# A two-layer attention and MLP kernel: the first unit's maxima one quad further ahead, the second unit's rows in another room

## The chip, the cores and the metric

The kernel runs on one core of one Trainium2 chip. The metric is the device time of one execution in microseconds (us); the kernel before is shown by the median of its timed runs. Five engines work side by side, each through its own instructions in order: TensorE (PE; its weight loads are shown as PEld), VectorE (DVE), ScalarE (ACT), GpSimd (POOL) and SyncE (SP), which here only issues DMAs. ACT issues the DMAs of the weights.

## The reference

The input has 2048 rows of 640 numbers. The same two blocks are applied twice, with the same weights both times:

```python
x = x + attention(layernorm(x), wqkv, wo)     # 32 heads of 20, sliding window of 256 keys
x = x + mlp(layernorm(x), w1, b1, w2, b2)     # 640 -> 1536 -> 640
```

In the attention, q, k and v are the three thirds of `x @ wqkv`. Scores are q.k / sqrt(20); a query sees its own position and the 255 before it; the softmax is taken over these, its weighted sum of v is formed, and the heads together are multiplied by `wo`. In the MLP, `h = x @ w1 + b1`, negative values become zero, the rest is squared, and `h @ w2 + b2` is the result. All is float32.

## The kernel before

**Units.** The 2048 rows are cut into 8 groups of 256 (`T`), and with two layers there are 16 units (`NU`), worked through in order. For a unit u the work is: layernorm of its 256 rows (two blocks of 128), q and k (`stage_qk`) and v (`stage_v`), the attention in eight "quads" of four heads, the projection by `wo` (`stage_o`), the second layernorm, and the MLP (`stage_f`). The first unit of a layer has no earlier keys and uses "whole" quads (`whole_quad`); the others use "half" quads (`halves_quad`).

**Numbers as pairs.** A float32 operand of a large matrix multiplication is kept as two float16 parts, high and low, and three products are added (`mm3`, line 339). Every result that becomes an operand again is therefore evicted twice: ACT writes the high part, then DVE writes the low part (lines 534 and 537 for q and k). The weights are split in the same way when they have been loaded (lines 271 and 272).

**The quads.** For each quad four passes of TensorE alternate:
- "m" (`max_quad`): scores, of which DVE takes the maximum over the keys (lines 717, 720; lines 683 for whole quads);
- "r" (`max_out`): the maxima of two quads are turned by TensorE and written by SP into two extra rows of q (line 757), so that they are subtracted inside the next scores;
- "s" (`exp_quad`): the scores again, now less their maximum; ACT takes the exponential (line 825), and POOL and DVE clear what lies outside the window;
- "v" (`pv_quad`): the weighted sum of v (line 931), copied out by ACT (line 943), for half quads added up by DVE (line 946), and written to device memory every second quad (line 951).

m and s share the same banks of the accumulation memory. The large multiplications ("dense" work) use two other banks; a new one waits until a bank's eviction is done. `load_o` reads a unit's attention result back from device memory (lines 984, 985), divides by the row sums (1017, 1020), and splits it (1024, 1027) for `stage_o`.

**Trips.** q and k of a unit go from their evicted form (`qd`) to device memory (`leave`, lines 583 and 585) and back in another layout (line 589).

**Rows of the next units.** A layernormed block has to be turned for the projections. `split_t` does it with TensorE transposes (line 403) and two evictions (lines 389, 390). `cross` does it with two casts (ACT line 452, DVE line 456) and DMA transposes issued by SP (line 459). Before the change units 1 and 2 go by `cross` (`ln_early`).

**Rooms.** Several tiles share memory over time. `hraw` (name stg) is the room that holds the MLP's hidden values later; at first it has two sides of equal size, side 0 and side 1. `kts[2]`, later the k of unit 2, holds at first some of the loaded `wqkv`, then unit 1's turned rows (`place`), then the second-layer MLP weights `w2` as they come in, five places in all, two of them elsewhere. The tile "qd" is one room for several purposes. Before the change the loads of `w2` into `kts[2]` wait for `gate2`, which opens once v of unit 1 has been computed.

**The order of the work.** The kernel writes its order out by hand with a small planner in Python, which runs while the program is built. Each instruction off TensorE is a `Job` with an engine, an assumed cost, earlier jobs it needs and an urgency (a lower number goes first). The planner keeps an assumed clock per engine and places a job on its engine when it could start (`pump`). The urgencies are in the dictionary `urgency`: `od` the split of the attention result, `ln` the layernorms of `stage_o`, `turn` the maxima, `exp` and `clear` the exponentials and clearing of half quads, `y` and `cross` the ways of the turned rows, `out` the evictions. "Bulk" jobs, the loads of `wo`, `w1` and `w2` on ACT, are also paced by what DMA is assumed to be under way (`moved`).

For unit 0 the function `flow` takes a list of passes (`todo`) and draws dense work from the generator `ahead_all` (units 0 to 2: q, k, v) whenever the next pass isn't ready. What is then left of `ahead_all` is worked off in unit 1. From unit 1 on, `together` lays the dense work of a unit between its quads: the projections of unit u + 1, `stage_o` and `stage_f` of unit u - 1. In the last two units some dense work is held back (`CARRY` from unit 14 into 15, `KEEP` past the quads of unit 15) to cover the last trip of the attention result. `LEAD` is 3: the maxima run three quads ahead.

The core of the old order, lines 1364 to 1366:

```python
todo = [("m", n) for n in range(GQ)] + [("r", 0)] + [("m", n) for n in range(GQ, LEAD)]
for n in range(NQ):
    todo += [("s", n)] + ([("r", n + LEAD - GQ)] if n % GQ == 1 else []) + [("m", n + LEAD), ("v", n)]
```

with `GQ` = 2 and `NQ` = 8.

Of the kernel before, what the change touches and what calls it, by code (L numbers as in the profile page):

```python
# [16 lines left out]
P = 128  # L17
# [28 lines left out]
def kernel(ctx: ExitStack, tc: tile.TileContext, x, wqkv, wo, w1, b1, w2, b2, out):  # L46
# [71 lines left out]
    TAIL = {"A": 115.0, "D": 85.0, "G": 40.0, "S": 0.0}  # L118

    class Job:  # L120
        def __init__(self, eng, cost, fn, deps, nb, prio, size=0, idle=False, land=LAND):
# [4 lines left out]
        def ready(self):  # L126
            return all(d.end is not None for d in self.deps)

        def start(self):
            t = max([clk[self.eng], self.nb] + [d.end + LAT for d in self.deps])  # L130
            return max(t, moved[0] - 2200.0) if self.idle else t

# [186 lines left out]
    def load_w2():  # L319
        used_by = {}  # L320
        for c, place in enumerate((3, 4, 0, 1, 2, 0, 1, 2, 0, 1, 2, 0)):
            first = [w1j[f] for f in (c // 4 * 2, c // 4 * 2 + 1, 6 + c // 4 * 2, 7 + c // 4 * 2)]
            st = vts[1 + place][1][:, :D] if place > 2 else krow[2][:, D * place:D * (place + 1)]
            load = bulk(lambda st=st, c=c: nc.scalar.dma_start(st, w2[c * P:(c + 1) * P, :]), P * D * 4,
                        *([w2j[used_by[place]]] if place in used_by else [gate] if place > 2 else [gate, gate2]))
            w2j[c] = convert(st, w2_s[:, 0, c], w2_s[:, 1, c], D, load, *first)
            used_by[place] = c
        sums.extend(post("D", 130, lambda i=i: set_sums(4 + i), w2j[used_by[3 + i]], prio=2) for i in range(2))

    urgency = {"out": 0, "od": 1, "cross": 1, "mask": 0, "turn": 1, "exp": 1, "ln": 1, "y": 0.5, "clear": 0.5}

# [108 lines left out]

    def cross(ys, dst, room, prio=2):

        box = {}
        js, out, j = [], [], None
        for i, (y, ready) in enumerate(ys):
# [12 lines left out]

            j = post("A", 615, high, ready, j, prio=prio)
            out.append(dma(lambda turn=turn: turn(0), P * D * 2, j, cost=1250.0, land=CROSS))
# [4 lines left out]
    def ln_early(u, place=None):  # L467

        def dst():
            yTs[u] = place  # L470
            if place is None:
                yTs[u] = sb.tile([P, 2, KC, T], F16, name="yT", tag="yT", bufs=1)
            return yTs[u]

        pre[u] = cross(lns.pop(u), dst, lambda: hraw[:, KC * T:2 * KC * T].bitcast(F16).rearrange(
            "p (i a n) -> p i a n", i=2, a=2), 1)
        left["side1"] = ((0, -u), pre[u], [])

# [23 lines left out]
    def stage_qk(u, which=(0, 1)):  # L502
# [9 lines left out]
        for j, c0 in order:  # L512
            if j not in qds:
                if j == 0:
                    qts[u] = sb.tile([P, NP, T], F16, name="qt", tag="qt", bufs=2)
                if j and u < 2:
                    qd, k = side(0), "side0"
                elif u == 2 and not j and opened0:
                    qd, k = side(1), "side1"
                elif j and u > 2:  # L520
                    qd = beside(u)[:, 1].rearrange("p (c a n) -> p c a n", a=2, n=T)
                    k = None
                else:
                    qd, k = sb.tile([P, KC, 2, T], F16, name="qd", tag="qd", bufs=1), "qd"
# [15 lines left out]
            def evict(wait, k=k, n=n, c0=c0, high=high, low=low, jobs=jobs, j=j, dst=dst, qd=qd):  # L540
                pr = urgency["out"]
                old = left.get(k, ())
                if k and (j, u) != old[:1]:
                    old = left[k] = ((j, u), [], old[1] if old else [])
# [28 lines left out]
    def leave(u, j, dst, qd, ready, c0, n):  # L573
# [17 lines left out]

        wrote = dma(write, n * P * 3 * T * 2, ready, n=2, prio=0)

# [375 lines left out]
    def load_o(u, late=False, free_=()):  # L969
# [16 lines left out]

        loaded = dma(load, P * (KC + 1) * T * 4, *wrote, *free_, n=2, prio=0)
        if u == NU - 1:
            both = sb.tile([P, 2, D], F32, name="x1", tag="qt", bufs=2)
# [308 lines left out]

    QKC, VC, OC, FCST, LNC, CARRY, KEEP, MID = 16.4e3, 8.2e3, 8.2e3, 39.2e3, 1.2e3, 18e3, 24e3, 10e3

    def flow(todo, dense):
# [3 lines left out]
        while todo:  # L1305
# [19 lines left out]
            elif kind == "s":  # L1325
                quad = exp_quad(n)
            else:
                pv_quad(n, quad)
            pump()
# [17 lines left out]

    place = kts[2].rearrange("p a n -> p (a n)")[:, :2 * KC * T].rearrange("p (a c n) -> p a c n", a=2, n=T)

    def ahead_all():  # L1350
        yield from stage_qk(0)
        ln_early(1, place)
        yield from stage_v(0, range(2))
        ln_load(2)
        yield from stage_v(0, range(2, 4))
        ln_early(2)
        yield from stage_qk(1)
        yield from stage_v(1)
        gate2.end = now[0]
        yield from stage_qk(2)  # L1360
        yield from stage_v(2)

    rest = ahead_all()
    todo = [("m", n) for n in range(GQ)] + [("r", 0)] + [("m", n) for n in range(GQ, LEAD)]
    for n in range(NQ):
        todo += [("s", n)] + ([("r", n + LEAD - GQ)] if n % GQ == 1 else []) + [("m", n + LEAD), ("v", n)]
    flow(todo, rest)
# [3 lines left out]
    while not all(j.end is not None and j.end <= now[0] + LOOK for j in bbjobs):  # L1371
        c = next(rest)
        if not isinstance(c, Want):
            used[0] += c
            step(c)
    left_over = 3 * (QKC + VC) - used[0]
    rate[0] = 320.0
    for u in range(1, NU):
        last = u == NU - 1
        if u == 1:  # L1380
            urgency.update({"out": 0, "od": 1.5, "cross": 1, "mask": 0, "turn": 0.7, "exp": 0.7, "ln": 0.5, "y": 1, "clear": 0.5})
        quads, ahead = range(NQ * u, NQ * (u + 1)), range(NQ * u + LEAD, NQ * (u + 1) + LEAD)
# [46 lines left out]
```

## Time and profile before

| | us |
|---|---|
| timed runs | 1559.91, 1560.23, 1561.74 |
| median | 1560.23 |
| the profiled execution | 1561.46 |
| its span, first to last instruction | 1559.6 |
| TensorE busy in the span | 1533.5 |
| DVE busy | 1043.3 |
| ACT busy | 669.7 |
| POOL busy | 451.8 |

The span is that of the instructions; the profiled execution's time has 1.9 us more around it. The mean granted clock of TensorE is 0.997. Rows of the timeline read: start, duration, engine, line, operation, what is written from what, shapes, how many instructions were merged (x), and in brackets the idle time of the engine before it and what ended that. Rows of a table by stretch read: from:to, length, then for TensorE, its weight loads, DVE, ACT and POOL the busy time with the number of instructions, the granted clock, the DMA engines' share and GB/s. Rows of the waits read: who waited for whom, the total in us, how often, and the longest.

### The profile page before, as it was taken

The numbers are of one execution on the slowest core, as the hardware profiler recorded it, in microseconds if no ns is written. First come the engines' busy times: TensorE is split into PE (matmuls) and PEld (weight loads), VectorE is DVE, ScalarE is ACT, GpSimd is POOL, SyncE is SP. The second block draws the span as 40 slices with busy tenths as digits, with TensorE's granted clock in tenths as the row PEclk, the third lists the DMA queues.
The fourth block names the chain that finished last, engine by engine and source line by source line (L and its number), as shares of the span: only waits on it lengthen the run. The fifth ranks groups of instructions, "written<-read, shape, count | busy, mean of one in ns | idle before, by whom it ended". The sixth has DMA issues, their size and how long they took to land. (4 is left out here: it accounts for less than half of the span.)

```text
span 1559.6 us, 58897 instructions
## 1 busy us (share of the span) xinstructions
PE 1533.5 (98%) x25822; PEld 1198.6 (77%) x25822; DVE 1043.3 (67%) x2244; ACT 669.7 (43%) x1365; POOL 451.8 (29%) x847
## 2 busy tenths in 40 slices
PE   8998999999999999999999999999999999999999
PEld 6666778787787877878777787877878777786777
DVE  8878775666757667675666757667675676667642
ACT  4565435334453443435343453444435335354422
POOL 1223314232141331413224141321413214142412
PEclk9999999999999999999999999999999999999999
DMA  9975354352534424344462434425243342542120
GB/s 271 209 201 127 80 121 92 106 114 54 123 88 114 105 74 126 69 126 89 99 130 63 119 91 119 100 70 132 67 126 89 94 117 65 122 90 59 30 68 18
DMA packets 248745, 162.16 MB, mean 104 GB/s; under 512 B 96552, under 2 KB 232232, under 8 KB 248488
## 3 DMA queue, kind: packets, MB, share of 16 engines
q1 hardware_dynamic: 242120, 148.89, 38.7%
q10 hardware_dynamic: 6368, 9.50, 2.1%
q8 instruction: 202, 3.31, 0.9%
q14 instruction: 55, 0.45, 0.1%
HBM read 84.68 MB, written 52.95 MB: 88 GB/s over the span
## 5 line engine op out<-in xcount | busy, mean ns | idle before, releaser
L825 ACT ACTIVATE pt<-bb 128x640 f32<-128x640 f32 (+2 forms) x512 | 311.9, 684 | 167.6 <-PE bb L840 148.9
L854 POOL TENSOR_SCALAR_AFFINE_SELECT pt<-pt 64x256 f32<-64x256 f32 x448 | 199.3, 445 | 582.1 <-ACT pt L825 560.0
L339 PE MATMUL acc<-y,w_s 128*128 128x256 f16 x2880 | 330.2, 274 | 1.2 <-DVE y L390 1.2
L339 PE MATMUL acc<-w_s,hh 128*128 128x320 f16 (+1 forms) x2340 | 326.7, 297 | 0.1
L339 PEld LDWEIGHTS <-w_s 128*128 128x128 f16 x2880 | 276.4, 98 | 40.9 <-issue 2.0
L339 PEld LDWEIGHTS <-hh 128*128 128x128 f16 x2340 | 222.1, 98 | 86.8 <-issue 0.4
L720 DVE TENSOR_REDUCE mx<-bb 128x4 f32<-128x1024 f32 x224 | 273.2, 1224 | 6.8
L339 PE MATMUL acc<-yT,wq_s 128*128 128x256 f16 x2250 | 259.1, 273 | 3.0 <-DVE qd L537 1.2
L339 PEld LDWEIGHTS <-wq_s 128*128 128x128 f16 x2400 | 229.6, 98 | 37.3 <-issue 4.3
L863 DVE COPY_PREDICATED_SCALAR pt<-drop,zero 128x256 f32 x224 | 99.9, 497 | 134.3 <-ACT pt L825 133.8
L1130 DVE TENSOR_TENSOR hh<-r,hh 128x256 f16<-128x256 f32 x192 | 98.3, 525 | 110.8 <-ACT hh L1127 105.7
L931 PE MATMUL pv<-pt,vt 64*32 64x192 f32 (+5 forms) x3840 | 166.7, 302 | 0.9 <-DVE y L390 0.6
L943 ACT COPY ot<-pv 128x256 f32<-128x256 f32 x128 | 47.6, 372 | 276.1 <-PE bb L931 247.2
L1124 POOL TENSOR_TENSOR r<-r 128x256 f32<-128x256 f32 x192 | 121.9, 655 | 127.9 <-ACT r L1120 125.3
L931 PE MATMUL bb<-pt,vt 64*32 64x128 f32 (+3 forms) x3584 | 153.5, 301 | 0.0
L717 DVE COPY_PREDICATED bb<-maskq,bb 128x256 f32<-128x256 uint16 x224 | 93.8, 423 | 85.7 <-PE bb L703 80.0
L931 PEld LDWEIGHTS pv<-pt,vt 64*32 64x32 f32 (+1 forms) x3840 | 125.5, 106 | 31.7 <-issue 3.7
L339 PE MATMUL acc<-wo_s,od 128*128 128x320 f16 x960 | 139.6, 299 | 2.2 <-ACT od L1024 2.0
L339 PE MATMUL acc<-wq_s,yT 128*128 128x320 f16 x900 | 132.1, 302 | 5.0 <-DVE qd L537 4.2
L1120 ACT ACTIVATE r<-acc,b1s 128x256 f32<-128x256 f32 x192 | 81.1, 476 | 98.6 <-PE acc L339 96.5
L339 PEld LDWEIGHTS <-od 128*128 128x128 f16 x960 | 90.9, 98 | 40.6 <-ACT od L1024 2.3
L339 PEld LDWEIGHTS <-yT 128*128 128x128 f16 x900 | 87.1, 98 | 40.0 <-issue 6.2
(103 smaller groups left out, 1476.3 us busy)
## 6 DMA issues: line engine op xcount, KB each, us to landing
qt<-qk SPq DMA_DIRECT2D x30, 480.0 KB
kt<-qk SPq DMA_DIRECT2D x30, 480.0 KB
o<-ot SPq DMA_DIRECT2D x256, 42.0 KB
qk<-qd SPq DMA_DIRECT2D x15, 640.0 KB
od<-o SPq DMA_DIRECT2D x14, 640.0 KB
qk<-yl SPq DMA_DIRECT2D x13, 640.0 KB
xt<-in_A_x_dram SPq DMA_DIRECT2D x16, 320.0 KB
x<-in_A_x_dram SPq DMA_DIRECT2D x16, 320.0 KB
```

What stands on the lines that cost most here:

```text
L339: nc.tensor.matmul(acc, lhs(a, c), rhs(b, c), start=(k == 0), stop=(k == 3 * nk - 1))
L717: nc.vector.copy_predicated(wins[:, :, 4 * Q:], later, wins[:, :, :Q])
L720: nc.vector.tensor_reduce(most, wins[:, :, Q:], axis=mybir.AxisListType.X, op=ALU.max)
L825: return lambda: nc.scalar.activation(room_of(box)[:, a:b], bank[:, a:b], AF.Exp, scale=SCALE / (QS * QS))
L854: nc.gpsimd.affine_select(out=m, in_=m, pattern=[[0, 4], [-1 if k else 1, Q]], base=0, fill=0.0, compare_op=ALU.is_gt if k else ALU.is_ge, ...
L863: nc.vector.copy_predicated(m, drop[:, k:k + 1, :].bitcast(mybir.dt.uint16).to_broadcast([P, 4, Q]), zero.unsqueeze(1).to_broadcast([P, 4, ...
L931: nc.tensor.matmul(pv[h][32 * jj:32 * (jj + 1), q0 * Q:(q0 + w) * Q], vf[r, c:c + 32], boxes[e]["pt"][r, a:b], start=(k == 0), stop=(k == ...
L943: nc.scalar.copy(ot[:, qd % 2], to)
L1120: nc.scalar.activation(box["r"], acc[:, f, :], AF.Relu, bias=b1s[:, f0 + f:f0 + f + 1], scale=1.0 / (YS * WS))
L1124: nc.gpsimd.tensor_tensor(box["r"], box["r"], box["r"], op=ALU.mult)
L1130: nc.vector.tensor_sub(hh[:, 1, f, :], box["r"], hh[:, 0, f, :])
```

## The change

- In unit 0 the maxima run four quads ahead instead of three (m0 to m3 and two "r" before s0; none beside the last quad); "r" follows "v".
- Unit 1's rows are turned by TensorE (`ln_t`) between two halves of v of unit 0, and lie in side 1 of `hraw` instead of `kts[2]`. The rows of unit 2 still go by `cross`, now through the "qd" room.
- Q of unit 2 uses side 0 instead of side 1 of `hraw`, where it comes before the attention result of unit 0 is loaded.
- The loads of `w2` into `kts[2]` wait for the split of `wqkv` instead of `gate2`.
- `quiet`: from the last "v" of unit 0 until its attention result has been loaded, the planner issues no bulk load and no write of unit 2's q and k.
- K of unit 1 is asked for after Q of unit 1 and the casts of unit 2.
- The urgencies are other ones, and their update comes at unit 2 instead of unit 1; `CARRY` and `KEEP` are 20 and 28 instead of 18 and 24.

```diff
+    quiet = []
...
         def ready(self):
-            return all(d.end is not None for d in self.deps)
+            return all(d.end is not None for d in self.deps) and not (self.idle and any(q.end is None for q in quiet))
...
-            return max(t, moved[0] - 2200.0) if self.idle else t
+            return max([t, moved[0] - 2200.0] + [q.end for q in quiet]) if self.idle else t
...
-                        *([w2j[used_by[place]]] if place in used_by else [gate] if place > 2 else [gate, gate2]))
+                        *([w2j[used_by[place]]] if place in used_by else [gate] if place > 2 else [gate, *wqj.values()]))
...
-    urgency = {"out": 0, "od": 1, "cross": 1, "mask": 0, "turn": 1, "exp": 1, "ln": 1, "y": 0.5, "clear": 0.5}
+    urgency = {"out": 0, "od": 1, "cross": 2, "mask": 0, "turn": 1, "exp": 0.5, "ln": 1, "y": 0.5, "clear": 0}
...
-            j = post("A", 615, high, ready, j, prio=prio)
+            j = post("A", 615, high, ready, j, *free_, prio=prio)
...
-        pre[u] = cross(lns.pop(u), dst, lambda: hraw[:, KC * T:2 * KC * T].bitcast(F16).rearrange(
-            "p (i a n) -> p i a n", i=2, a=2), 1)
-        left["side1"] = ((0, -u), pre[u], [])
+        pre[u] = cross(lns.pop(u), dst, lambda: sb.tile([P, 2, 2, D], F16, name="yl", tag="qd", bufs=1), 1, left["qd"][1])
+        left["qd"] = ((0, -u), pre[u], [])
...
                 elif u == 2 and not j and opened0:
-                    qd, k = side(1), "side1"
+                    qd, k = side(0), "side0"
...
-        wrote = dma(write, n * P * 3 * T * 2, ready, n=2, prio=0)
+        wrote = dma(write, n * P * 3 * T * 2, ready, *(quiet if u == 2 else ()), n=2, prio=0)
...
+        if u == 0:
+            loaded.gates.append(quiet[0])
...
-    QKC, VC, OC, FCST, LNC, CARRY, KEEP, MID = 16.4e3, 8.2e3, 8.2e3, 39.2e3, 1.2e3, 18e3, 24e3, 10e3
+    QKC, VC, OC, FCST, LNC, CARRY, KEEP, MID = 16.4e3, 8.2e3, 8.2e3, 39.2e3, 1.2e3, 20e3, 28e3, 10e3
...
+                if n == NQ - 1:
+                    quiet.append(Job("S", 0.0, None, [], 0.0, 0))
                 pv_quad(n, quad)
...
-    place = kts[2].rearrange("p a n -> p (a n)")[:, :2 * KC * T].rearrange("p (a c n) -> p a c n", a=2, n=T)
+    place = hraw[:, KC * T:2 * KC * T].bitcast(F16).rearrange("p (a c n) -> p a c n", a=2, n=T)

     def ahead_all():
         yield from stage_qk(0)
-        ln_early(1, place)
         yield from stage_v(0, range(2))
-        ln_load(2)
+        yield from ln_t(1, place)
+        ln_load(2, prio=1)
         yield from stage_v(0, range(2, 4))
+        yield from stage_qk(1, (0,))
         ln_early(2)
-        yield from stage_qk(1)
+        yield from stage_qk(1, (1,))
         yield from stage_v(1)
-        gate2.end = now[0]
         yield from stage_qk(2)
         yield from stage_v(2)
...
-    todo = [("m", n) for n in range(GQ)] + [("r", 0)] + [("m", n) for n in range(GQ, LEAD)]
+    todo = [("m", n) for n in range(GQ)] + [("r", 0)] + [("m", n) for n in range(GQ, LEAD + 1)] + [("r", GQ)]
     for n in range(NQ):
-        todo += [("s", n)] + ([("r", n + LEAD - GQ)] if n % GQ == 1 else []) + [("m", n + LEAD), ("v", n)]
+        m = n + LEAD + 1
+        todo += [("s", n)] + [("m", m)] * (n < NQ - 1) + [("v", n)] + [("r", m)] * (m % GQ == GQ - 1 and n < NQ - 1)
...
-        if u == 1:
-            urgency.update({"out": 0, "od": 1.5, "cross": 1, "mask": 0, "turn": 0.7, "exp": 0.7, "ln": 0.5, "y": 1, "clear": 0.5})
+        if u == 2:
+            urgency.update({"out": 0, "od": 1, "cross": 0.5, "mask": 0, "turn": 0.5, "exp": 0.5, "ln": 1, "y": 1, "clear": 0.5})
```

More of the change, by code (lines that the diff above doesn't have):

```diff
@@ L441, in ln_t, with cross @@
             yield from split_t(ys[i][0], yT[:, :, :, i * P:(i + 1) * P], ys[i][1], pre[u], bb[i])
-    def cross(ys, dst, room, prio=2):
+    def cross(ys, dst, room, prio=2, free_=()):
         box = {}
@@ L542, in evict @@
                 old = left.get(k, ())
-                if k and (j, u) != old[:1]:
+                if k and (not old or old[0] != (j, u)):
                     old = left[k] = ((j, u), [], old[1] if old else [])
@@ L1375 @@
             step(c)
-    left_over = 3 * (QKC + VC) - used[0]
+    left_over = 3 * (QKC + VC) + LNC - used[0]
     rate[0] = 320.0
```

## The prediction

> **What bounds the kernel now.** I read the page's busy table first, then who TensorE waited for, in two stretches, and then the granted clock where the waits lie.
>
> ```profile
> span 1559.6 us, 58897 instructions
> PE 1533.5 (98%) x25822; PEld 1198.6 (77%) x25822; DVE 1043.3 (67%) x2244; ACT 669.7 (43%) x1365; POOL 451.8 (29%) x847
> ```
>
> TensorE is busy for 98% of the span. Whatever the diff does elsewhere, it can only win where TensorE waits or is clocked down. The waits of TensorE from 20 to 165 us (the three longest), and after "..." from 165 to 1400 us (those of 0.5 us or more):
>
> ```profile
> PE acc L339 <- DVE qd L537: 5.3, 3, 4.2
> PE tr L403 <- DVE xt L378: 1.8, 1, 1.8
> PE bb L840 <- DVE ot L946: 1.3, 1, 1.3
> ...
> PE bb L840 <- issue: 2.3, 3, 1.1
> PE bb L703 <- ACT pt L825: 0.9, 2, 0.7
> PE acc L339 <- DVE yl L537: 0.5, 2, 0.3
> ```
>
> The second group sums to 3.7 us over 1235 us: units 2 to 13 are full, and the diff can hardly win there. The first group has 8.4 us in 145 us. The clock (the number after the five engines' busy times; DMA share and GB/s follow) shows two further losses:
>
> ```profile
> 34.60:38.00 3.40, 3.40 (x16) 1.98 (x15) 2.27 (x14) 0.44 (x1) 0.00 (x0) 0.55 1.00 241
> 140.40:147.20 6.80, 6.44 (x63) 4.71 (x63) 5.77 (x12) 3.93 (x7) 2.24 (x2) 0.52 0.10 18
> ```
>
> From 34.6 to 38.0 us the clock is 0.55, which loses 3.4 x 0.45 = 1.5 us; from 140.4 to 147.2 it is 0.52, which loses 6.8 x 0.48 = 3.3 us. Each follows a stretch in which TensorE stood: the longest wait for L537 (4.2 us, up to 33.06 by a row below), and the 1.8 us wait for L378 with its neighbours. So two stalls hold what can be won: **stall 1** 4.2 + 1.5 = 5.7 us, **stall 2** 1.8 + 1.3 + 3.3 = 6.4 us.
>
> **The change part by part.** The sum is made against the profiled execution's own 1561.46 us (its span of 1559.6 and 1.9 around it), which is 1.23 us above the median of the three timed runs, 1560.23; I carry the difference over to the median.
>
> *Stall 1: unit 1's rows leave the DMA path.* The rows of ACT, DVE, TensorE and SP, in this order, at that place:
>
> ```profile
> 31.09 0.72 ACT L452 CAST stg<-xt 128x640 f16<-128x640 f32 x1 [2.76 <-DVE xt L378]
> 31.72 0.38 ACT L534 ACTIVATE qd<-acc 128x256 f16<-128x256 f32 x1
> ...
> 30.44 0.61 DVE L378 TENSOR_SCALAR xt<-xt,bmv 128x640 f32<-128x640 f32 x1 [0.44 <-POOL bmv L376]
> ...
> 32.59 0.42 DVE L537 SCALAR_TENSOR_TENSOR qd<-acc,qd 128x256 f16<-128x256 f32 x1
> ...
> 33.06 0.70 PE L339 MATMUL acc<-wq_s,yT 128*128 128x320 f16 x4 [4.18 <-DVE qd L537]
> ...
> 28.35 4.69 SPq L459 DMA_TRANSPOSE kt<-stg x3
> ```
>
> V's first matmul (33.06) needs a bank, whose eviction is the ACT half L534 and then the DVE half L537. L534 stands behind the cast L452 of unit 1's second row block, and that cast stood 2.76 us for the layernorm's L378. The diff takes both casts of unit 1 (L452), their DVE halves (L456) and four DMA transposes off this place: unit 1 is now turned by TensorE (ln_t), after two quarters of V(0). L534 can then run when its matmul ends, at 33.06 - 4.18 = 28.9. Best case: 0.38 + 0.42 and hand-offs, a stall of 1.1 us. Worst: DVE still has L378 (ends 31.05) ahead of two L537, a stall of 2.8. I take 1.9, between the two, since nothing says on which side L378 falls: 2.3 us won of the wait (1.4 to 3.1). Of the clock's 1.5 I take half (0 to 1.5). **Won: 3.1 us (1.4 to 4.6).** SP also gets back the 4.69 us of the first three transposes, which stood ahead of unit 0's own q and k loads; I count that at nothing, as the first quads wait for the loads issued before them.
>
> [...]
>
> *What the transposes cost.* TensorE's transposes of unit 0's first block for the MLP (three and two chunks), and the mean evictions of such a tile on ACT and DVE:
>
> ```profile
> 134.91 0.49 PE L403 MATMUL tr<-ident,xt 128*128 128x128 f32 x3
> ...
> 136.02 0.44 PE L403 MATMUL tr<-ident,xt 128*128 128x128 f32 x2
> ...
> L390 DVE TENSOR_TENSOR y<-tr,y 128x384 f16<-128x384 f32 (+1 forms) x8 | 3.7, 485 | 1.3 <-ACT y L389 1.3
> ...
> L389 ACT CAST y<-tr 128x384 f16<-128x384 f32 (+1 forms) x8 | 3.3, 427 | 6.1 <-PE tr L403 3.9 <-DVE x L1056 2.0
> ```
>
> Two blocks cost 2 x (0.49 + 0.44) = 1.9 us of TensorE, on the path, since TensorE is the bound. Four tiles share two banks: the third, the fourth and the next accumulation each wait for 0.43 + 0.49 less the other tile's 0.44, so 0.5 each, 1.4 in all at worst without hand-offs, 2.1 with them, nothing if something else is placed between. I take 0.7. **Lost: 2.6 us (1.9 to 4.0).**
>
> *Maxima one quad further ahead.* This moves work and removes none; it is worth only what dense work (projections of units 1 and 2) is still in hand when unit 1 begins. The starts of the score passes s1 to s6, SP's load of unit 1's K, and m8, the first maxima of unit 1:
>
> ```profile
> 56.22 0.72 PE L886 MATMUL bb<-qt,kt 62*128 62x256 f16 x8
> ...
> 65.44 0.50 PE L886 MATMUL bb<-qt,kt 62*128 62x256 f16 x8
> ...
> 71.45 0.50 PE L886 MATMUL bb<-qt,kt 62*128 62x256 f16 x8
> ...
> 80.06 0.50 PE L886 MATMUL bb<-qt,kt 62*128 62x256 f16 x8
> ...
> 85.29 0.82 PE L886 MATMUL bb<-qt,kt 62*128 62x256 f16 x8
> ...
> 93.24 0.50 PE L886 MATMUL bb<-qt,kt 62*128 62x256 f16 x8
> ...
> 76.90 1.20 SPq L589 DMA_DIRECT2D kt<-qk x2
> ...
> 87.56 1.03 PE L703 MATMUL bb<-kt,qt 60*64 60x256 f16 x38
> ```
>
> Steps to even quads, which also wait for rows of maxima, take 9.2, 8.6 and 8.0 us; to odd ones 6.0 and 5.2. The rows now come a quad sooner, so three steps could each save some 2.7 us, 8 in all. Against that, a fourth pass of maxima stands before s0 (about 2 us later, an estimate: a third of a step of 6), and m8 is now wanted right after s4, near 75 us, when K(1), loaded at 76.90 now, cannot be there; the K(1) matmuls come behind the transposes. So I take 2 us of the 8 (0 to 6) by which v7, the last work of unit 0's quads, ends sooner.
>
> *Stall 2: what is in hand when unit 0's layernorm is late.* SP's load of the attention result, the last projection of unit 2, the first by that result, and the transposes that waited:
>
> ```profile
> 110.26 0.59 SPq L984 DMA_DIRECT2D rs<-o x1
> ...
> 119.39 2.20 PE L339 MATMUL acc<-wq_s,yT 128*128 128x320 f16 x15 [0.28 <-DVE mT L795]
> ...
> 122.54 1.80 PE L339 MATMUL acc<-wo_s,od 128*128 128x320 f16 x12
> ...
> 140.24 1.30 PE L403 MATMUL tr<-ident,xt 128*128 128x128 f32 x5 [1.78 <-DVE xt L378]
> ...
> 115.00:120.00 5.00, 4.72 (x68) 3.24 (x67) 4.71 (x11) 2.34 (x6) 0.00 (x0) 1.00 1.10 315
> ```
>
> The projections of unit 2 ended at 121.6, so at 136 to 140 nothing was left to fill the wait. From load to first use are 12.3 us, in which the DMA engines ran at up to 1.10 of their share (last row) on weights and unit 2's q and k. The `quiet` job holds both back until the load has landed, behind nothing but themselves: I take 2 us off the 12.3 (0 to 4). With the 2 us from v7, 4 us of dense work are left to lay over a wait of 1.8. If they lie there, 1.8 + 3.3 = 5.1 us are won; the 1.3 us for L946 is a DVE queue matter and stays. I take three quarters. **Won: 3.8 us (0 to 6.4).** The held-back weights have no cost while this slack stands:
>
> ```profile
> 157.36 1.97 DVE L272 SCALAR_TENSOR_TENSOR w_s<-kt,w_s 128x640 f16<-128x640 f32 x2
> ...
> 172.97 0.76 PE L703 MATMUL bb<-kt,qt 60*64 60x256 f16 x38
> ```
>
> The last second-layer weight is converted at 159.3, and the maxima that need its room for unit 2's K start at 172.97; the weights may now also start before the projections of unit 1 are done, so this moves sooner.
>
> *Side effects.* Q and K of unit 2 now share the "qd" room if Q comes after the load; K's eviction then waits for Q's write, which waits for `quiet`. Quads can run meanwhile: **lost 0.5 us (0 to 3)**, the upper end being an estimate, half of a quad's step of 6 us, the other half of which is the quad's own work. Urgencies: the new values of cross, exp and clear act on nothing in unit 0, whose quads are whole ones; from unit 2 on, layernorm goes from ahead of the maxima to behind them. Nothing counted, see the third rival. The carried work (18 to 20 us, 24 to 28 kept) takes 2 us of dense work from the last unit's quads:
>
> ```profile
> 1441.23 0.97 PE L339 MATMUL acc<-wo_s,od 128*128 128x320 f16 x4 [1.97 <-ACT od L1024]
> ```
>
> This wait of 1.97 may shrink as the projection comes later, another may grow: 0 (-2 to 2).
>
> *Sum:* 3.1 - 2.6 + 3.8 - 0.5 = 3.8 us won. 1561.5 - 3.8 = 1557.7 for an execution like the profiled one, and 1560.2 - 3.8 = **1556.4 us** for the median.
>
> **The rivals.**
>
> *Both stalls go.* Stall 1 gives 4.6, the transposes cost 1.9, stall 2 gives all 6.4: 9.1 us, **1551.1**. For it: the three steps to even quads hold 8 us of slack, twice what I use. Against it: K(1) is late for m8.
>
> *The first unit gets no shorter.* m8 waits for K(1), the dense work is drawn while it waits, stall 2 stays: 3.1 - 2.6 - 0.5 = 0, **1560.2**. This is also the case in which the change doesn't do what it says. For it: the load at 76.90 stands close before m8 today. Against it: the quieter load alone should leave 2 us in hand.
>
> *Slower: layernorm behind the maxima.* In a full unit (DVE, SP, TensorE):
>
> ```profile
> 516.83 0.60 DVE L378 TENSOR_SCALAR xt<-x,bmv 128x640 f32<-128x640 f32 x1
> ...
> 522.03 1.23 SPq L459 DMA_TRANSPOSE y<-yl x1
> ...
> 529.35 2.90 PE L339 MATMUL acc<-y,w_s 128*128 128x256 f16 x25
> ...
> L720 DVE TENSOR_REDUCE mx<-bb 128x4 f32<-128x1024 f32 x224 | 273.2, 1224 | 6.8
> ```
>
> From the end of the last transpose's issue (523.26) to the MLP's start are 6.1 us, less its landing, which no row shows: between 0 and 6.1 in hand, and I take the middle, 3. If each of the layernorm's three DVE steps falls behind one more maximum (1.22), it is 3.7 us later, 0.7 too late; in 13 units 9 us, less the 3.8: **1566**. It decides from the point where the delay passes what is in hand. Against it: cross goes ahead at the same time, and quads can fill a hole of 0.7.
>
> *K of unit 2 stuck behind `quiet`*, with stall 2 as it is: 3.1 - 2.6 - 3 = 2.5 lost, **1563**.
>
> **How the numbers follow.** My forecast 0.44, both stalls go 0.20, no shorter 0.22, layernorm 0.09, K stuck 0.05. A measurement of this kernel tells about 0.2% (3.1 us) from no change, so faster means below 1557.1. My forecast's own range is 1553 to 1560, of which 0.32 lies below that and 0.12 within; of "no shorter" 0.03, 0.14 and 0.05 are faster, same and slower. Faster 0.32 + 0.20 + 0.03 = 0.55; same 0.12 + 0.14 = 0.26; slower 0.05 + 0.09 + 0.05 = 0.19. A range of 1550.5 to 1563 holds my forecast, half of the first rival, nearly all of the second and half of the last: about 0.8.
>
> **What would show it.** Stall 1: V's first matmul before 31.7 with less than 2.8 us idle before it, no 0.55 clock after. Transposes: ten L403 rows near 35 to 45 us, with under 2.1 us idle around them. First unit: steps to even quads at about 6 us, m8 near 80, v7 some 2 us sooner. Stall 2: projections of unit 2 still running after 122, and no half clock near 140. Rest: TensorE's waits from 165 to 1400 still near 4 us in all. I am wrong if m8 is as late as now, if the half clock near 140 stays, or if those waits grow by more than 4 us.

## The result: slower, and the profile after

The kernel after takes **1572.18 us** (median of 6 timed runs, 1570.69 to 1574.97) against 1560.99 us (1559.05 to 1564.36) for the kernel before beside it: a ratio of **1.0072, 95% interval 1.0057 to 1.0087**. The forecast was 1556.4 us, with a range up to 1563. The first fence shows the page's span and busy table of the profile after, and behind "..." TensorE's waits from 165 to 1400 us (who waited for whom, total us, how often, longest).

```profile
span 1569.6 us, 58932 instructions
PE 1536.6 (98%) x25832; PEld 1200.3 (76%) x25832; DVE 1046.0 (67%) x2246; ACT 671.7 (43%) x1367; POOL 445.2 (28%) x847
...
PE bb L841 <- DVE ot L947: 3.8, 5, 1.1
PE bb L841 <- issue: 2.7, 2, 1.5
PE bb L704 <- ACT pt L826: 2.5, 3, 0.9
```

TensorE is busy 3.1 us longer than before, while the span is 10.0 us longer. With five smaller rows not shown (3.1 us), the waits in the long middle sum to 12.1 us, against 4.0 before (the 3.7 of the three rows in the prediction, and 0.3). Their largest row hardly stood there before (0.3 us, once): the score pass "s" waits for L947, the addition behind a half quad, on DVE. Line numbers of the middle are one to three higher than in the kernel before.

Where the 10 us lie is read from the first score row of units 3 and 14, here of before (L840) and, after "...", of after (L841):

```profile
293.85 0.76 PE L840 MATMUL bb<-qt,kt 62*64 62x128 f16 x38
1334.74 1.04 PE L840 MATMUL bb<-qt,kt 62*64 62x128 f16 x38
...
293.98 0.76 PE L841 MATMUL bb<-qt,kt 62*64 62x128 f16 x38
1343.78 0.76 PE L841 MATMUL bb<-qt,kt 62*64 62x128 f16 x38
```

Units 0 to 2, which the change was mostly about, take 0.1 us more; units 3 to 13 take 1049.8 instead of 1040.9, **8.9 us more**; what follows takes 225.8 instead of 224.9. The loss is not spread evenly: by the first score rows of the units, unit 7, at whose end the layers change, takes 4.2 us more, units 5, 6, 9 and 12 take 1.1 to 1.6 us more each, and the other six together 0.8 less.

**The start.** Unit 1's transposes and the V of unit 0 (TensorE), in the profile after:

```profile
28.28 3.29 PE L341 MATMUL acc<-wq_s,yT 128*128 128x320 f16 x23
...
32.90 0.49 PE L405 MATMUL tr<-ident,xt 128*128 128x128 f32 x3
33.59 0.44 PE L405 MATMUL tr<-ident,xt 128*128 128x128 f32 x2 [0.20 <-ACT vt L623]
34.75 0.77 PE L405 MATMUL tr<-ident,xt 128*128 128x128 f32 x5 [0.73 <-DVE stg L392]
...
36.46 2.74 PE L341 MATMUL acc<-wq_s,yT 128*128 128x320 f16 x19 [0.49 <-DVE stg L392]
```

V starts at 28.28 with no idle time before it: stall 1 is gone, and the transposes cost 1.7 us and waits of 1.4. Then the first unit's end (SP, TensorE):

```profile
110.23 0.61 SPq L985 DMA_DIRECT2D rs<-o  x1
...
116.45 0.57 PE L341 MATMUL acc<-wq_s,yT 128*128 128x320 f16 x3
118.18 0.27 PE L704 MATMUL bb<-kt,qt 60*64 60x256 f16 x1 [1.16 <-ACT pt L826]
119.38 0.75 PE L704 MATMUL bb<-kt,qt 60*64 60x256 f16 x37 [0.93 <-ACT pt L826]
122.60 4.68 PE L341 MATMUL acc<-wo_s,od 128*128 128x320 f16 x30
...
137.43 0.74 PE L405 MATMUL tr<-ident,xt 128*128 128x128 f32 x5 [1.64 <-DVE xt L380]
```

The attention result is loaded at 110.23 (before: 110.26) and used at 122.60 (before: 122.54). So the quads of unit 0 ended no sooner, and the trip was no shorter. But the projections of unit 2 are done at 117.0 instead of 121.6: what stall 1 gave was used up by drawing the dense work sooner, and TensorE then waits for exponentials. The granted clock (the number after the engines' busy times) shows what followed these waits, 0.50 from 120.11 on, and another pair like it at the end of unit 1, with 0.50 from 195.20 on:

```profile
116.69:120.10 3.41, 1.32 (x44) 0.81 (x44) 3.33 (x9) 3.33 (x7) 1.71 (x3) 1.00 1.14 188
120.11:123.52 3.41, 3.41 (x70) 2.66 (x69) 2.32 (x7) 0.73 (x2) 0.74 (x1) 0.50 1.06 276
133.76:137.17 3.41, 2.00 (x69) 1.37 (x53) 3.34 (x10) 1.22 (x3) 0.55 (x1) 1.00 0.30 108
191.79:195.20 3.41, 1.60 (x45) 1.04 (x46) 1.30 (x3) 2.49 (x4) 1.66 (x4) 1.00 0.25 97
195.20:198.61 3.41, 3.41 (x69) 2.53 (x68) 2.44 (x5) 0.37 (x1) 0.00 (x0) 0.50 0.03 7
```

The half clock that stood at 34 and 140 us stands at 120 and 195 us now.

**A full unit.** Unit 5 starts at 485.2 before and at 484.3 after. The rows are SP's load of b2, POOL's first b2 addition and a score pass, and for after also a maximum, the second block's normalise and two low halves on DVE and SP's last transposes; first before (its L378 at 516.83 and its last transpose at 522.03 stand in the prediction), then after:

```profile
528.60 0.44 SPq L1069 DMA_DIRECT2D xt<-in_B_b_dram  x1
532.37 0.86 POOL L1076 TENSOR_TENSOR x<-x,xt 128x320 f32<-128x320 f32 x1 [6.81 <-DMA xt<-in_B_b_dram]
...
544.92 0.76 PE L840 MATMUL bb<-qt,kt 62*64 62x128 f16 x38
```

```profile
517.94 1.23 DVE L721 TENSOR_REDUCE mx<-bb 128x4 f32<-128x1024 f32 x1
...
519.71 0.61 DVE L380 TENSOR_SCALAR xt<-x,bmv 128x640 f32<-128x640 f32 x1
...
521.26 2.53 SPq L461 DMA_TRANSPOSE y<-yl  x2
...
528.22 1.25 SPq L1072 DMA_DIRECT2D xt<-in_B_b_dram  x1
534.33 0.86 POOL L1079 TENSOR_TENSOR x<-x,xt 128x320 f32<-128x320 f32 x1 [9.76 <-DMA kt<-qk]
...
540.43 1.43 DVE L1133 TENSOR_TENSOR hh<-r,hh 128x256 f16<-128x256 f32 x2 [1.93 <-ACT hh L1130]
...
545.43 0.75 PE L841 MATMUL bb<-qt,kt 62*64 62x128 f16 x37 [1.09 <-DVE ot L947]
```

Before, L378 came 31.6 us into the unit, ahead of two maxima; after, L380 comes 35.4 us into it, behind them. SP's last transposes are issued by 39.5 instead of 38.0 us into the unit. The load of b2, which stands behind them on SP, is issued 43.9 instead of 43.4 us into the unit and takes 1.25 us to issue instead of 0.44. POOL's first b2 addition starts at 50.0 instead of 47.2 into the unit. It stands ahead of the MLP's squares (L1127) on POOL; ACT's casts (L1130) and DVE's low halves (L1133) wait for these, the maxima and behind them the addition L947 stand behind DVE's low halves, and the score pass waits for L947. Unit 9 shows the same (50.0 instead of 47.8 us, an issue of 1.11 us); in units 6 and 12 the load is itself issued 1.0 and 2.0 us later into the unit.

### The profile page after: what moved, and what is told of

It is laid out like the page before. It is cut to its first block, busy times and chain, and to the rows that moved or that the text cites. A ratio compares the mean times of both kernels' runs of the same rounds, so it can differ in the third digit from the quotient of the medians.

```text
span 1569.6 us, 58932 instructions
## 1 busy us (share of the span) xinstructions
PE 1536.6 (98%) x25832; PEld 1200.3 (76%) x25832; DVE 1046.0 (67%) x2246; ACT 671.7 (43%) x1367; POOL 445.2 (28%) x847
## 4 chain that ended last, share of the span: by engine, by line
PE 80%; DVE 5%; DMA 3%; ACT 2%; issue 2%; POOL 2%; SPq 1%; ACTq 0%; POOLq 0%; DVEq 0%
PE acc L341 61%; PE pv L932 7%; PE bb L841 5%; PE bb L704 4%; PE bb L932 2%; DVE mx L721 1%; ACT pt L826 1%; DMA kt<-qk 1%; POOL r L1127 1%; POOL pt L855 1%; SPq L758 1%; DMA xt<-xs 1%; DVE bb L718 0%; DMA ov<-o 0%; DVE ot L947 0%
## 5 line engine op out<-in xcount | busy, mean ns | idle before, releaser
L932 PE MATMUL pv<-pt,vt 64*32 64x192 f32 (+5 forms) x3840 | 171.1, 305 | 2.2 <-DVE x L1162 1.2
L1133 DVE TENSOR_TENSOR hh<-r,hh 128x256 f16<-128x256 f32 x192 | 97.9, 525 | 106.9 <-ACT hh L1130 100.5
L932 PE MATMUL bb<-pt,vt 64*32 64x64 f32 (+3 forms) x3584 | 156.5, 304 | 1.1 <-DVE mx L684 1.1
L1127 POOL TENSOR_TENSOR r<-r 128x256 f32<-128x256 f32 x192 | 119.8, 644 | 119.6 <-ACT r L1123 116.9
L932 PEld LDWEIGHTS bb<-pt,vt 64*32 64x32 f32 x3584 | 117.8, 106 | 3.1 <-issue 1.8
```

The source lines that it names most:

```text
L932: nc.tensor.matmul(pv[h][32 * jj:32 * (jj + 1), q0 * Q:(q0 + w) * Q], vf[r, c:c + 32], boxes[e]["pt"][r, a:b], start=(k == 0), stop=(k == ...
L1127: nc.gpsimd.tensor_tensor(box["r"], box["r"], box["r"], op=ALU.mult)
L1133: nc.vector.tensor_sub(hh[:, 1, f, :], box["r"], hh[:, 0, f, :])
```

## The experiments

Unless another is named, the ratio is that of the timed runs to the kernel before on the same chip, with its 95% interval. "Units 3 to 13" is worked out from the first score rows of units 3 and 14, as above: 1040.9 before, 1049.8 after. In the ten other profiles that have the old values from unit 2 on it lies between 1039.3 and 1042.8, so smaller differences than that say little.

**The two tables of urgencies undone.** On the kernel after, both tables are as before, and the update comes at unit 1 again.

```diff
-    urgency = {"out": 0, "od": 1, "cross": 2, "mask": 0, "turn": 1, "exp": 0.5, "ln": 1, "y": 0.5, "clear": 0}
+    urgency = {"out": 0, "od": 1, "cross": 1, "mask": 0, "turn": 1, "exp": 1, "ln": 1, "y": 0.5, "clear": 0.5}
...
-        if u == 2:
-            urgency.update({"out": 0, "od": 1, "cross": 0.5, "mask": 0, "turn": 0.5, "exp": 0.5, "ln": 1, "y": 1, "clear": 0.5})
+        if u == 1:
+            urgency.update({"out": 0, "od": 1.5, "cross": 1, "mask": 0, "turn": 0.7, "exp": 0.7, "ln": 0.5, "y": 1, "clear": 0.5})
```

> The changed kernel with both urgency tables as before (the first one, and the update at unit 1). In the profile of the changed kernel, units 0 to 2 end 0.1 us later than before and the other 9.9 us are lost from unit 3 on: 4.2 in unit 7, about 1.4 each in units 5, 6, 9 and 12, 1.0 in the last two. Theory A (the urgencies from unit 2 on make that loss): 1562, within 3 us. Rival B (the new start only shifts the later units against their DMAs, and the loss comes with the start whatever the urgencies): 1570 to 1572. Rival C (unit 1's urgencies hide a gain of the start, 3 us ahead at s8 and lost again by s16): below 1558.

Measured: 1567.84 us, 1.0039 (1.0024 to 1.0054). Units 3 to 13 are back at 1042.8, but the last two units take 230.8 us instead of 225.8. So the urgencies make the loss of the middle, and something else is left.

**Only the update of the full units undone** (it stays at unit 2, with the old values).

> The changed kernel with the old urgency values from unit 2 on; unit 1 keeps the new ones. Theory A: the loss after unit 3 goes, 1562 to 1564. Rival B: 1570 to 1572. Against the run with all old urgencies it shows what unit 1's values are worth: nothing by theory A, some 3 us by rival C.

Measured: 1568.99 us, 1.0044 (1.0029 to 1.0059); units 3 to 13 at 1042.4.

**Only that update done.** On the kernel before, the new values from unit 2 on, and nothing else.

> The kernel before with nothing changed but the urgency values from unit 2 on, which are the new ones. Theory A: 1568 to 1571, with unit 7 some 4 us longer than before and several units 1 to 1.5 longer. Rival B: 1560 to 1562.

Measured: 1573.78 us, 1.0084 (1.0064 to 1.0105); units 3 to 13 at 1054.8. One line of the change by itself costs as much as the whole.

**CARRY and KEEP undone** on the kernel after (18 and 24).

> The changed kernel with CARRY and KEEP as before (18 and 24). Theory A and rival B: the last two units lost 1.0 us, so 1571, not to be told from the changed kernel. If the smaller amount of dense work in the last quads costs more than the profile shows: 1568 or less.

Measured: 1573.10 us, 1.0067 (1.0049 to 1.0085): beside the new urgencies the sizes decide nothing.

**Which of the values.** On the kernel before:

```diff
+        if u == 2:
+            urgency["ln"] = 1
```

> The kernel before with one urgency value changed: ln is 1 instead of 0.5 from unit 2 on, behind the maxima (0.7). Theory H (this value makes the loss in the full units: the second block's layernorm is normalised some 3 us later, behind two maxima, its DMA transposes go later on SP, and the load of b2 that stands behind them too): units 3 to 13 sum to 1046 to 1053 instead of 1041, 1566 to 1570. Rival I (cross, turn or od at their new values make it): 1560 to 1562.

Measured: 1574.49 us, 1.0084 (1.0069 to 1.0099). Units 3 to 13 take 1053.9 us. TensorE's waits from 165 to 1400 us in this kernel:

```profile
PE bb L840 <- issue: 6.3, 4, 1.9
PE bb L840 <- DVE ot L946: 4.6, 6, 1.1
```

On the kernel before, the layernorm behind the maxima brings the waits for L946 and the whole loss by itself: 13.0 us, where all of the new values together cost 13.9. The larger row, "issue", stands in the middle of a score pass some 26 us into units 4, 6, 10 and 12 (2.3 us before, 2.7 after); what it waits for, no row shows. On the kernel after, the reverse, `"ln": 0.4` from unit 2 on with `"cross": 0.5` kept:

> The changed kernel with one urgency value changed: ln is 0.4 instead of 1 from unit 2 on, ahead of the maxima (0.5) again. Theory H: the waits of s for L947 go but unit 7 stays long (98 instead of 94, which the run with cross behind took back), units 3 to 13 sum to 1044 to 1046, 1566 to 1568. Rival I: 1572.

Measured: 1573.48 us, 1.0067 (1.0050 to 1.0083). Units 3 to 13 come to 1047.3 only, unit 7 alone still takes 98.3 us (94.3 before), and the last two units 230.6. Against the expectation the waits for L947 stay:

```profile
PE bb L841 <- DVE ot L947: 3.9, 5, 1.1
```

And with `"cross": 1` and `"ln": 1`:

> The changed kernel with one value undone: cross is 1 from unit 2 on, so the low parts and casts of the rows to be turned go behind the maxima again. Theory E (unit 7 is 4.2 us longer because two layernorms and their casts stand ahead of the maxima on DVE, and the load of b2 goes later on SP behind the transposes): unit 7 back at 94 to 95, 1566 to 1568. Rival F (layernorm's value 1 does it): 1572.

Measured: 1571.54 us, 1.0049 (1.0034 to 1.0064); unit 7 is back at 95.1, but units 3 to 13 take 1049.3, and the waits for L947 are 4.0 us in seven. So both values do harm, in different places, and on the kernel after undoing one alone doesn't take the loss away. The value of `cross` costs unit 7 some 3.4 us, where the profiles with the old values lie between 94.3 and 95.0. That of `ln` costs the ten other units: they take 949.0 us with the layernorm ahead, close to the 945.0 to 948.5 of the old values, but 951.3 with it behind, and 954.2 with `cross` behind as well. The other values were not tried by themselves. The place of `cross`, in the profile after, is the change of layers (DVE and TensorE):

```profile
760.97 0.83 DVE L458 TENSOR_TENSOR yl<-xt,yl 128x640 f16<-128x640 f32 x1
...
761.11 0.59 PE L932 MATMUL pv<-pt,vt 64*32 64x256 f32 x2 [1.20 <-DVE x L1162]
762.85 0.37 PE L932 MATMUL bb<-pt,vt 64*32 64x256 f32 x1 [1.15 <-DVE mx L684]
767.00 0.75 PE L841 MATMUL bb<-qt,kt 62*64 62x128 f16 x37 [0.90 <-DVE ot L947]
```

The next layer's rows are normalised and cast by DVE ahead of the clearing and the maxima of the quad that runs, and TensorE waits three times, 3.3 us in all.

**Is it the b2 load?** b2 is loaded once, into a tile of its own, instead of once per unit through SP's queue.

```diff
-        b2s = sb.tile([P, D], F32, name="xt", tag="xt", bufs=2)
-        load = dma(lambda: nc.sync.dma_start(b2s, bass.AP(tensor=b2.tensor, offset=b2.offset, ap=[[0, P], [1, D]])),
-                   P * D * 4)
+        if "b2" not in kept:
+            kept["b2"] = sb.tile([P, D], F32, name="b2all")
+            kept["load"] = dma(lambda: nc.sync.dma_start(kept["b2"], bass.AP(tensor=b2.tensor, offset=b2.offset,
+                                                                             ap=[[0, P], [1, D]])), P * D * 4)
+        b2s, load = kept["b2"], kept["load"]
```

On the kernel after:

> The changed kernel with b2 loaded once into a tile of its own instead of once a unit, so that POOL's additions of b2 never stand for a DMA in units 2 to 15. Theory G (in a full unit the waits of s for L947 come when POOL starts these additions later than 49.4 us into the unit, and behind them the squares, the low halves, the maxima): these waits of about 1.1 us in units 5, 9 and 12 go, 4 us or more in all, 1568 or less. Rival (the order of DVE alone makes them): 1572, waits as before.

Measured: 1568.19 us, 1.0028 (1.0014 to 1.0043); units 3 to 13 at 1043.1, so 6.7 of the 8.9 us are back, with every urgency as in the change. Outside unit 7 nothing of the loss is left (946.4 us, 946.6 before); unit 7 keeps 2.4 of its 4.2. So outside unit 7 the new order does its harm through the b2 load. The edit also takes b2 out of the two tiles "xt" that it shares with the layernormed rows, which was not tried by itself. The row of the waits for L947 from 165 to 1400 us falls from 3.8 us in five waits to

```profile
PE bb L841 <- DVE ot L947: 0.9, 1, 0.9
```

The 14 profiles that load b2 in every unit bear it out, over units 3 to 13 without unit 8, 140 in all. Take how far into its unit the first b2 addition starts, less TensorE's waits (of 0.2 us or more) 20 to 35 us into the unit. All 31 units in which that is 49.0 us or more have a wait of TensorE 58 to 66 us in, of up to 1.09 us in all; of the 102 in which it is under 48.9, none has one, and the seven between are mixed.

On the kernel before:

> The kernel before with b2 loaded once. Theory G: the old order has the load 0.5 us sooner and hardly waits, so little is won: 1559 to 1561. If a time below 1558 is measured, the load cost the old order too.

Measured: 1559.97 us, 0.9984 (0.9973 to 0.9995); units 3 to 13 at 1039.8, so with the old urgencies the load costs these units about 1 us at most, which is within the spread named above.

**The new start alone.** The kernel after with the old values from unit 2 on and the old CARRY and KEEP; unit 1 has the new urgencies.

> The new start alone: unit 1's urgencies new, the old ones from unit 2 on, CARRY and KEEP as before. Theory D (old urgencies with the new CARRY and KEEP lose 6 us in the last unit, as the profile of the run before with old values from unit 2 shows: unit 14 and the rest together 230.9 us against 224.9): 1561 to 1563, the same as before, since units 0 to 2 ended at 293.9 with and without the new start. Rival (the 6 us come from the new start's shift, not from CARRY and KEEP): 1567 to 1569.

Measured: 1565.51 us, 1.0015 (1.0005 to 1.0026). Still no gain. From this kernel parts were taken out one by one. The old list of passes (three quads ahead):

> The new start alone with the old list of passes: maxima three quads ahead, not four. The new start alone was 0.15% slower than before. Theory J (the list does nothing for unit 1: v7 ended 1.6 us later with it, and unit 0's projection began at 122.6 as before): 1565, as the new start alone. Rival: the longer lead is what pays for the transposes, and without it 1568 or more.

Measured: 1568.93 us, 1.0043 (1.0028 to 1.0058). Without `quiet`:

> The new start alone without quiet: bulk loads and unit 2's writes go as they come. Theory J (the trip of unit 0's result took 12.4 us with quiet against 12.3 before, so quiet is worth nothing): 1565, as the new start alone. Rival: quiet holds back unit 2's q and k and the dense work runs out sooner for it; without it 1562 or less.

Measured: 1568.36 us, 1.0039 (1.0024 to 1.0054). Unit 1's rows by `cross` and DMA transposes again (`ln_early(1, place)` where `ln_t` stands):

> The new start alone, but unit 1's rows go by casts and DMA transposes as before, at the place in the order where the TensorE transposes stood. Theory K (the ten transposes and the waits around them cost the 3 us predicted and more, since the first stall is gone by the place in the order, not by the way): units 0 to 2 end 2 to 3 us sooner, 1561 to 1562. Rival L (by DMA the rows come later, K of unit 1 and m8 with them): 1566 or more.

Measured: 1586.97 us, 1.0161 (1.0144 to 1.0178). At the new place the DMA way leaves TensorE standing:

```profile
54.59 5.53 PE L341 MATMUL acc<-stg,wq_s 128*128 128x256 f16 x25 [14.72 <-DMA stg<-yl]
```

So within the new start, with unit 1's new urgencies, each part earns its place, against the first theory for each: by the ratios the lead 0.28%, `quiet` 0.24%, the transposes 1.46%. The reverse, `quiet` and the kept b2 on the kernel before:

> The kernel before with quiet and with b2 loaded once, nothing else. b2 loaded once gave 0.16% (2.5 us) on it. If quiet shortens the trip of unit 0's attention result as it does in the new start (2.5 us): 1556 to 1558. If it only helps where the dense work of unit 2 comes after the trip: 1560, as with b2 alone.

Measured: 1578.78 us, 1.0108 (1.0093 to 1.0123). The second MLP weights then come too late in unit 1, likely because the new rooms are missing, which was not tried by itself:

```profile
182.15 0.42 PE L341 MATMUL acc<-w_s,hh 128*128 128x320 f16 x1 [5.08 <-ACT w_s L273]
```

**The new start with all of the old urgencies**, in unit 1 too, and the old CARRY and KEEP: the first experiment's edit and `CARRY, KEEP` at 18 and 24.

> The new start with all urgencies as before, unit 1's too, and CARRY and KEEP as before. The earlier run with all old urgencies ended units 0 to 2 some 1.5 us sooner than the one with unit 1's new ones, at an equal number of half-clock windows. If that holds: 1 to 2 us below the new start alone, 1562 to 1564. If unit 1's urgencies do nothing: 1565.

Measured: 1559.20 us, 0.9989 (0.9977 to 1.0001), 0.26% less than with the new urgencies in unit 1. The waits for exponentials near 193 us are gone: from 165 to 300 us no wait of TensorE is listed. Against the first experiment only CARRY and KEEP differ, and those show at the end. TensorE's transposes for the last MLP, first in the kernel with 20 and 28, then the last MLP's start with 18 and 24, which waits for nothing:

```profile
1520.68 1.05 PE L405 MATMUL bb<-ident,xt 128*128 128x128 f32 x5 [3.35 <-DVE xt L380]
```

```profile
1514.58 19.94 PE L341 MATMUL acc<-y,w_s 128*128 128x256 f16 x180
```

With 20 and 28, nothing is left to lay over the last layernorm; with 18 and 24, dense work of the unit before runs up to the MLP's start. The last two units take 230.8 and 224.8 us: 6 us.

**The best of both**: the same with b2 kept.

> The new start (unit 1 turned by TensorE, longer lead, quiet, rooms) with all of the old urgencies and the old CARRY and KEEP, and b2 loaded once into a tile of its own. Without the b2 edit this kernel took 1559.2 us (ratio 0.9989); the b2 edit alone took the kernel before to 0.9984. Theory A (the two gains lie in different stretches and add): 1556 to 1558, ratio 0.996 to 0.998. Theory B (with layernorm ahead of the maxima units 3 to 13 lose nothing to the b2 load any more, and what the b2 edit won on the kernel before was the start's spread between executions): 1558.5 to 1560.5, ratio 0.9985 to 1.000, units 3 to 13 at 1040 to 1042 either way.

Measured: 1560.88 us against 1563.3 for the kernel before, 0.9985 (0.9975 to 0.9996); units 3 to 13 at 1040.9. The two small gains don't add. This kernel, and the kernel before with b2 kept, are about 0.15% shorter than the kernel before, with intervals that end just below 1: the best of all the kernels, and less than the 0.2% that the prediction took as the bound.

## Why the prediction was wrong

**Stall 1: right, and more.** 3.1 us were forecast, 4.6 at most; the 4.2 us wait and the half clock behind it (1.5) are both gone, 5.7 (the clock is 1.00 from 34.77 to 38.19 us).

**The transposes: right.** 2.6 us forecast, 1.7 + 1.4 = 3.1 measured.

**Maxima further ahead: wrong.** The step said that v7, the last "v" of unit 0, ends 2 us sooner. The first score pass and v7 before, and then the first score pass, SP's load of unit 1's K, m8 and v7 after:

```profile
47.61 0.27 PE L886 MATMUL bb<-qt,kt 62*128 62x256 f16 x1 [0.36 <-DMA qt<-mT]
...
103.05 1.08 PE L931 MATMUL pv<-pt,vt 128*32 128x256 f32 x16
```

```profile
52.28 0.50 PE L887 MATMUL bb<-qt,kt 62*128 62x256 f16 x8
...
73.61 1.08 SPq L590 DMA_DIRECT2D kt<-qk  x2
...
83.28 0.76 PE L704 MATMUL bb<-kt,qt 60*64 60x256 f16 x38
...
104.65 0.98 PE L932 MATMUL pv<-pt,vt 128*32 128x256 f32 x16 [0.48 <-DVE qd L538]
```

v7 starts 1.6 us later. Two terms were mis-sized. The first pass comes 4.7 us later, not 2. The steps to s2, s4 and s6 take 8.7, 6.2 and 7.3 us, 3.6 less than before in all (8 were possible), and that to s1 2.7 less, but those to s3, s5 and s7 take 3.8 more. m8 does come sooner, 83.28 for 87.56, with K in place. That the lead is what delays v7 shows in the new start: with the old list s0 comes at 46.23 and v7 at 100.40, with the new one at 51.87 and 104.26. Yet unit 3 starts 2.0 us sooner with the new one (296.18 for 298.14), so what the lead wins, it wins in unit 1 and not where the step had it.

**Stall 2: the step that failed in the start.** 2 us from `quiet` and 2 from v7 were to lie over the wait. Neither came: 12.4 us from load to use, 12.3 before, and without `quiet` in the new start 12.4 as well, so its 0.24% lies elsewhere. The half clock at 140 us went, as foretold, but not for the reason given: the wait itself stays (1.64 us for 1.78). TensorE was idle 2.06 us from 136.67 to 140.08 before, and the clock behind that was 0.50; after, it is idle 1.41 us from 133.76 to 137.17, and the clock behind that is 1.00 (last section). And the dense work ran out sooner, so other waits came at 118 us with a half clock (0.50) behind them. Unit 1's urgencies, which the prediction did not price, add the waits at 193 us. Counting half of each half-clock stretch as lost (an estimate), unit 3 starts at 293.85 - 5.1 = 288.7 before, 290.6 after, 291.1 with the new start and unit 1's new urgencies, and 290.4 - 1.7 = 288.7 with the old ones. So the new start is worth nothing by itself, and unit 1's urgencies cost 2 us. Which of their values does it was not tried.

**Urgencies: the main failure.** "Nothing counted" was the term for the full units; it measured 8.9 us. Of the three signs of being wrong this one came: the waits from 165 to 1400 us grew by 8.1 us, where 4 was the limit. The third rival had the mechanism, layernorm behind the maxima, its delay (3.7 us; 3.8 in unit 5) and nearly the size (9 us; 1566 us in all, though its own terms add up to 1565), but it had 0.09, and its place was wrong: the MLP doesn't start later for lack of turned rows, it starts 44.1 us into unit 5 in both kernels. The size was partly luck: it was 0.7 us in each of 13 units, where five units lost 9.7 us and 4.2 of that is unit 7, mostly by `cross`. The work that was late next is the load of b2, behind the transposes on SP, and with it POOL's additions ahead of the squares. The row was there before, among POOL's waits from 293 to 1335 us:

```profile
POOL x L1076 <- DMA xt<-in_B_b_dram: 68.2, 10, 8.2
```

POOL already stood for that load in ten of these eleven units. The rival's argument against ("cross goes ahead at the same time") fell in unit 7, which that value costs 3.4 us (98.5 against 95.1); the 2.9 us that it gives back in the ten others are within the spread. What makes 0.5 us of later issue 2.9 us on POOL in unit 5 is open: the issue itself took 0.8 us longer, and the transfer that the profile names for the wait is that of k, issued behind it.

**CARRY and KEEP: 0 (-2 to 2)** held beside the new urgencies, and was wrong by 6 us beside the old ones. The 0.5 us for unit 2's rooms has no run of its own.

In sum, 3.8 us won were forecast and 10.0 lost in the profiles: 8.9 in the full units, which the prediction had set at nothing, 0.9 in the last two, and the start's gain taken back within it.

## What to carry to other kernels

A changed priority acts in every repetition; here five units of eleven paid 1 to 4 us each, which outweighs the repair of the start. Price it by following, from the moved instruction, each in-order queue that it delays, to the next engine that stands there already (here SP's small load and POOL's wait for it). Work that saves time in a stretch whose filler is finite only moves the hole unless what ends the stretch also comes sooner. Sizes, priorities and placements tuned together have to be tried together: three parts of this change (`CARRY` and `KEEP`, the layernorm's urgency, `quiet`) gain or lose several us depending on the others.

## What the runs showed of the hardware

**Where the half clock lay.** In the profiles before and after, each half-clock stretch of the span lasts 3.413 us or twice that (6.827), and all changes of the granted clock lie whole steps of 3.413 us behind its first record (at 6.94 and 7.46 us). The clock of two more profiles was read in the same steps, counted from 5.50 (old urgencies) and 4.73 us (start, all urgencies old): up to 1395 us each step has 1.00 or 0.50 throughout. A window is one such step. The half-clock stretches, by the number of steps ahead of them (the last of the old urgencies was read as 0.55 from 1521.70 to 1528.50):

```
before                      8, 39 (two windows)
after                       33, 55
old urgencies               9, 34, 36, 444 (two windows)
start, all urgencies old    35
```

Two windows in the profile before, of which the second comes right ahead of a half-clock stretch:

```profile
27.45:30.86 3.41, 1.43 (x14) 1.13 (x12) 2.85 (x8) 0.73 (x1) 1.47 (x1) 1.00 0.90 231
30.86:34.27 3.41, 1.21 (x13) 0.67 (x13) 2.21 (x6) 1.28 (x3) 0.00 (x0) 1.00 0.98 170
```

In these four profiles, up to 1395 us, eight windows have TensorE idle for 1.8 us or more, and seven are followed by a window at half clock (the one at 27.45, with 1.98 us idle, isn't); of eleven with 1.2 to 1.5 us idle (rounded to a tenth), one is (the one at 32.81 with the old urgencies, 1.42 us; windows that are at half clock themselves aside). So how much idle time goes ahead of a half clock, these windows don't settle. Behind two waits of 0.9 us in one window (up to 195.20, after; 1.81 us idle in all) a window at 0.50 follows, another 1.7 us if half of it is counted as lost (an estimate); behind a wait of 1.64 us, 1.4 of it in one window (133.76 to 137.17, after), the clock is 1.00.

**The same instructions, two starts.** The kernels with CARRY and KEEP at 20 and 28 and at 18 and 24 give TensorE the same instructions up to unit 14. Unit 3 starts at 294.09 in the one and at 290.37 in the other:

```profile
36.22:39.63 3.41, 3.41 (x15) 1.92 (x14) 2.64 (x17) 0.00 (x0) 0.00 (x0) 0.50 1.14 247
121.55:124.96 3.41, 3.23 (x64) 2.21 (x62) 2.71 (x7) 0.23 (x2) 0.00 (x0) 0.50 1.11 216
128.38:131.79 3.41, 3.41 (x15) 1.96 (x13) 2.38 (x5) 1.10 (x2) 0.00 (x0) 0.50 0.81 195
```

```profile
124.20:127.61 3.41, 3.38 (x13) 1.96 (x14) 1.73 (x4) 1.55 (x3) 0.00 (x0) 0.50 0.93 236
```

Three windows at half clock against one: counting half of each as lost (an estimate), 2 x 1.7 = 3.4 of the 3.7 us. A single profile can't tell starts apart that differ by less than this; the timed ratios, each over several executions, tell more.
